# One product of block 1 of the second MLP in the two-level form, with its input fold ahead of the other

## The chip, the cores and the metric

One core of a Trainium2 chip. The metric is the device time of one launch in microseconds (us). The runs of the kernel before gave 652.52 us as their median, between 652.52 and 653.16 us.

## The reference

Attention over 2 x 8 heads (576 positions, head size 64), once on means of 4 neighbouring positions and once on a band of 7, then an MLP with an ELU, then a second MLP with four experts. The change touches only the last:

```python
def _moe2_ref(x, domain_probs, w1, w2) -> np.ndarray:   # x 1152 x 512, w1 4 x 512 x 1024, w2 4 x 1024 x 512
    p = domain_probs / (domain_probs.sum(-1, keepdims=True) + 1e-09)
    for e in range(E):
        h = np.maximum(x @ w1[e], 0.0)
        out += p[:, e:e + 1] * (h @ w2[e])
```

All values are float32. The kernel splits each operand in a high and a low part and takes three matmuls (high x high, low x high, high x low) for one product (`mm3`, L232).

## The kernel before

**Blocks.** The second MLP goes through eight blocks of 512 of the hidden columns, two for each expert. A block n has a first layer (x times a 512 x 512 piece of `w1`) and a second layer (nine token tiles of 128 tokens, `l2e`, which add into `oacc`). The first layer is a Strassen product: seven products of quarter-size matrices. Block 0 has a form of its own (`quad`). From block 1 on the three products numbered 0, 1 and 3 come first, then the remaining ones (`ready`, `last`).

**Two forms of a product.** `plain(n, p)` computes a product of a 2 x 2 arrangement of 128-column pieces directly: four results, each of two `mm3` (6 matmuls of 128x288) in a fresh PSUM bank `psA`, each read once by ScalarE (product 0) or by a VectorE add (products 1 and 3). `inner(n, p)` applies the Strassen form once more: seven groups of one `mm3` (3 matmuls), on three banks: `psA` (called `pa`, four groups accumulate in it one after another), `psB` (`pb`, two groups) and `psC` (one). Between two groups in `pa` VectorE reads what is there so far. `inner` needs the folded input `xq[p]`, made by `fold(p)`: two VectorE sums (L1163), four VectorE differences (L1166), then four results, each a ScalarE copy and a subtraction of VectorE (the first) or GpSimd (L1171); and folded weights, made by `T` (four GpSimd operations, L965 to L968), `H(p, 1)` (a ScalarE copy) and `L(p, 1)` (a GpSimd subtraction). Block 1 has three plain products; block 2 and the later ones have three inner ones, and the folds of 0 and 1 for these are made during block 1. fold() writes its fourth result over a part of its input.

**Order.** Every engine runs its instructions in the order in which the program emits them. Two generators are woven: `weave` takes a step of the first layer at each "m" of a pattern and a step of the second layer's tiles at each "g". A step advances a counter, the emission clock: 0.8 for six matmuls of a product, 0.4 for three, 0.68 for three of a tile. Other work is in a list `due` of (count, function): before each step, all entries whose count is reached are emitted. `plan` puts weight steps in this list: F and F2 (loads), H, L, S, T, HS, LS, H2, L2. The counter starts at 0 with block 0's `quad`s (four of 7 x 0.8, and two tiles of 4 x 0.68 among them), and block 1 follows.

**Buffers.** `s8` is a set of equal SBUF slots, `st_pool[0]` and `st_pool[1]` are single buffers for folded weights, cA, cB and cC hold the sums of the products 0, 1 and 3, and `psb_` has eight PSUM banks given out in turn.

Of the kernel before, what the change touches and what calls it, by code (L numbers as in the profile page):

```python
# [151 lines left out]
def attn_moe_kernel(  # L152
# [794 lines left out]
    def w1_two(n, st_pool):  # L947


        e, s = sbs[n]  # L950
        mine = wm.setdefault(n, ({}, {}))[0]
        c = s * SB
        sub, add = ALU.subtract, ALU.add
        tt = nc.gpsimd.tensor_tensor
        raw, sts = [], {}

        def F():
            raw.append(s8.tile([P, KD, SB], F32, name="raw1", uses=5))
            nc.sync.dma_start(raw[0], w1[e, :, c:c + SB].rearrange("(k p) f -> p k f", p=P))

        def view():
            return raw[0].rearrange("p (h k) (j i f) -> p h k j i f", h=2, j=2, i=2)

        def sums(st, a11, a12, a21, a22):
            tt(out=st[0], in0=a21, in1=a22, op=add)  # L965
            tt(out=st[1], in0=st[0], in1=a11, op=sub)
            tt(out=st[2], in0=a11, in1=a21, op=sub)
            tt(out=st[3], in0=a12, in1=st[1], op=sub)  # L968

        def block(p):  # L970
            h, i = ((0, 0), (1, 0), None, (1, 1))[p]
            return view()[:, h, :, :, i]

        def T(*ps):
            pool = st_pool[0 if len(ps) > 1 else 1]
            st = pool.tile([P, 4, len(ps), P], F32, tag="st", name="st")
            for i, p in enumerate(ps):
                sts["w", p] = st[:, :, i]
            if len(ps) > 1:
                x = view()[:, :, :, :, 0]  # L980
                sums([st[:, o] for o in range(4)], x[:, :, 0, 0], x[:, :, 1, 0], x[:, :, 0, 1], x[:, :, 1, 1])
            else:
                x = block(p)
                sums([st[:, o, 0] for o in range(4)], x[:, 0, 0], x[:, 1, 0], x[:, 0, 1], x[:, 1, 1])

        def parts(p, o):
            w = mine["w", p]
            if o:
                return w[:, 0, 4:8], w[:, 1, 4:8], sts["w", p]
            return [w[:, m, 0:4].rearrange("p (k j) f -> p k j f", k=2) for m in range(2)] + [block(p)]  # L990

        def H(p, o):
            if o == 0:
                mine["w", p] = s8.tile([P, 2, 8, P], F32R, name="wq", uses=1)
            hi, _, x = parts(p, o)
            nc.scalar.activation(hi, x, AF.Copy)  # L996

        def L(p, o):
            hi, lo, x = parts(p, o)
            tt(out=lo, in0=x, in1=hi.bitcast(F32), op=sub)  # L1000
            if o == 0:
                s8.done(raw[0])

        def S(j):
            x = view()[:, :, :, j]
            f0, f1 = [[x[:, h, :, i] for h in range(2)] for i in range(2)]
            for o, a, b, op in (
                (f1[1], f1[0], f1[1], add), (f1[0], f0[0], f1[0], sub), (f0[0], f1[1], f0[0], sub), (f0[1], f0[1], f0[0], sub)
            ):
                tt(out=o, in0=a, in1=b, op=op)  # L1010

        def HS(j):
            mine["s", j] = w = s8.tile([P, 2, KD, 2 * P], F32R, name="ws", uses=2)
            nc.scalar.activation(w[:, 0], raw[0][:, :, 2 * j * P:2 * (j + 1) * P], AF.Copy)  # L1014

        def LS(j):
            w = mine["s", j]
            tt(out=w[:, 1], in0=raw[0][:, :, 2 * j * P:2 * (j + 1) * P], in1=w[:, 0].bitcast(F32), op=sub)  # L1018
            s8.done(raw[0])

        return dict(F=F, T=T, H=H, L=L, S=S, HS=HS, LS=LS)

    with ExitStack() as ph2:
# [130 lines left out]
        def fold(p):  # L1154

            xq[p] = up.tile([P, 3, 2, HB], F32R, tag=f"xq{p}", name="xq")
            buf = cC if p == 3 else up.tile([P, 4, HB], F32, tag=f"xq{2 * p + 1}", name="fold")
            f = buf.rearrange("p (a k) b -> p a k b", a=2)
            f11, f21, f12, f22 = (f[:, a, k] for a in range(2) for k in range(2))
            tt = nc.vector.tensor_tensor  # L1160
            for pair in range(2):
                x = (xbo, xbo, None, xto)[p][pair][:, p].bitcast(F32)
                tt(out=f[:, pair], in0=x[:, 0], in1=x[:, 1], op=add_)  # L1163
                yield
            for o, a, b in ((f11, f12, f11), (f12, f22, f12), (f22, f22, f11), (f21, f21, f22)):
                tt(out=o, in0=a, in1=b, op=sub)  # L1166
                yield
            for k, t in ((0, f11), (1, f22), (2, f12), (3, f21)):
                h, l = xin(p, k)
                cp(h, t)  # L1170
                (nc.gpsimd if k else nc.vector).tensor_tensor(out=l, in0=t, in1=h.bitcast(F32), op=sub)  # L1171
                yield

        def plain(n, p):

            w = wm[n][0]["w", p]
            o = {0: cA, 1: cB, 3: cC}[p]
            for pair in range(2):
                for j in range(2):
                    q_ = 2 * j + pair  # L1180
                    b = bank("psA")
                    for kk in range(2):
                        mm3(b[:, :HB], (w[:, 0, 2 * kk + j], w[:, 1, 2 * kk + j]), xsrc(p, kk, pair), kk == 0, kk == 1)
                    if p == 0:
                        cp(o[:, q_], b[:, :HB])
                    else:
                        add(o[:, q_], cA[:, q_], b[:, :HB])
                    psb_.done(b)
                    if q_ == 3:
                        s8.done(w)  # L1190
                    yield 0.8
# [131 lines left out]
        def join(*gs):  # L1323
            for g in gs:
                yield from g
# [16 lines left out]
        for n, at in ((0, 4), (2, 8), (3, 8.8), (1, 9.6)):  # L1342
            due += [(at, False, lambda n=n: first_xt(n))]
        plan(
# [4 lines left out]
        )  # L1349
        for p, at in (  # L1350
            (0, (28, 28.7, 29.4, 30.1, 30.8, 31.5, 32.2, 32.4, 32.6, 36)),
            (1, (36.5, 37.2, 38, 38.7, 39.4, 40.1, 41, 41.2, 41.4, 45)),
        ):
            due += [(t, False, lambda g=g: next(g)) for g in [fold(p)] for t in at]
        due.sort(key=lambda x: x[0])
# [6 lines left out]
        for n in range(len(sbs)):  # L1362
            m = n + 1
            if n:
                if m < len(sbs):
                    plan(
                        (0, m, "T", 0, 1), (0.5, m, "H", 0, 0), (0.6, m, "L", 0, 0), (4.5, m, "H", 0, 1),
                        (4.6, m, "L", 0, 1), (5, m, "T", 3), (11.6, m, "H", 1, 0), (11.7, m, "L", 1, 0),
                        (11.8, m, "H", 3, 0), (11.9, m, "L", 3, 0), (12, m, "H", 1, 1), (12.1, m, "L", 1, 1),
                        (12.5, m, "H", 3, 1), (12.6, m, "L", 3, 1), (12.7, m, "S", 0), (12.8, m, "S", 1),  # L1370
                        (24.5, m, "HS", 0), (24.6, m, "LS", 0), (25.5, m, "HS", 1), (25.6, m, "LS", 1), (27.5, m, "F2"),
                        (33.5, m, "H2", 0), (33.6, m, "L2", 0), (36.2, m, "H2", 1), (36.3, m, "L2", 1), (36.4, m + 1, "F"),
                    )
                weave(last(n, 0), tiles(n - 1, (6, 7, 8) if n > 1 else (7, 8)), "mgmgmgmgmgmg")
                weave(last(n, 1), tiles(n, (0, 1)), "mgmgmgmgmgmg")
            if m == len(sbs):
                weave(tiles(n, range(2, NTT)), iter(()), "")
                break
            if m == 1:
                pre = join(plain(1, 0), plain(1, 1), plain(1, 3), ready(1))  # L1380
                weave(pre, tiles(0, (2, 3, 4, 5, 6)), "mg" * 20)
                continue
            if m == 2:
                due += [(clock[0] + t, False, lambda g=g: next(g)) for g in [fold(3)] for t in (0, 0.9, 1.8, 2.7, 3.6, 4.5, 5.6, 6.2, 6.8, 7.4)]
                due.sort(key=lambda x: x[0])
                pre = join(inner(2, 0), inner(2, 1), inner(2, 3), ready(2))
                way = "mmmgmmgmggmg" "mmmgmmgmgm" "gmmmgmmgmggm" "mmgmmgmmgmm"
            else:
                pre = join(inner(m, 0), turns(inner(m, 1), inner(m, 3)), ready(m))
                way = "mmmgmmgmggmg" "mmmmgmmgmmgmmgmmgmmg" "mmgmmgmmgmgmg"  # L1390
            weave(pre, tiles(n, (2, 3, 4, 5)), way)
# [32 lines left out]
```

## Time and profile before

| | |
|---|---|
| median of the runs | 652.52 us (652.52 to 653.16) |
| profiled execution, its own time | 652.44 us |
| its span, first to last instruction | 650.6 us |
| TensorE busy | 644.1 us, 99% |
| VectorE busy | 450.3 us, 69% |
| GpSimd busy | 318.3 us, 49% |
| ScalarE busy | 302.9 us, 47% |

Times in the rows below are microseconds from the start of the span. PE is TensorE, PEld its weight loads, DVE VectorE, ACT ScalarE, POOL GpSimd, SPq the queue of SyncE, which issues the loads. A matmul's duration is that of one passage through the array; matmuls overlap, so the distance between the starts of two groups tells what a group occupies. A bracket at the end of a row is the idle time of the engine ahead of it and what ended it.

### The profile page before, as it was taken

The numbers are of one execution on the slowest core, as the hardware profiler recorded it, in microseconds if no ns is written. First come the engines' busy times: TensorE is split into PE (matmuls) and PEld (weight loads), VectorE is DVE, ScalarE is ACT, GpSimd is POOL, SyncE is SP. The second block draws the span as 40 slices with busy tenths as digits, with TensorE's granted clock in tenths as the row PEclk, the third lists the DMA queues.
The fourth block names the chain that finished last, engine by engine and source line by source line (L and its number), as shares of the span: only waits on it lengthen the run. The fifth ranks groups of instructions, "written<-read, shape, count | busy, mean of one in ns | idle before, by whom it ended". The sixth has DMA issues, their size and how long they took to land.

```text
span 650.6 us, 12345 instructions
## 1 busy us (share of the span) xinstructions
PE 644.1 (99%) x4800; PEld 592.2 (91%) x4800; DVE 450.3 (69%) x955; ACT 302.9 (47%) x825; POOL 318.3 (49%) x314
## 2 busy tenths in 40 slices
PE   9999999999999999999999999999999999999998
PEld 5789989999999999999988988988989989989887
DVE  5999999667668883776968666566566565656652
ACT  5999787456564656555323324133142243242110
POOL 5733352303233538386748848538458457376000
PEclk9999999999999999999999999999999999999999
DMA  9999730051141300020220301301102202102012
GB/s 245 220 227 186 168 96 1 2 195 66 65 130 65 130 2 1 2 65 1 65 65 1 129 1 25 106 0 66 66 2 64 66 1 68 62 1 66 1 48 98
DMA packets 40880, 46.70 MB, mean 72 GB/s; under 512 B 23030, under 2 KB 23286, under 8 KB 40822
## 3 DMA queue, kind: packets, MB, share of 16 engines
q1 hardware_dynamic: 40822, 45.91, 25.7%
q8 instruction: 38, 0.62, 0.4%
q14 instruction: 20, 0.16, 0.1%
HBM read 43.55 MB, written 2.36 MB: 71 GB/s over the span
## 4 chain that ended last, share of the span: by engine, by line
PE 87%; DVE 4%; ACT 3%; DMA 3%; POOL 2%; issue 1%; SPq 0%; ACTq 0%; DVEq 0%; POOLq 0%
PE psZ L240 30%; PE psH L240 16%; PE psY L240 14%; PE psE L240 7%; PE psA L240 6%; PE psG L240 3%; PE psF L240 3%; PE psB L240 2%; DMA raw<-in_moe_w_in_dram 2%; DMA raw<-in_k_dram 1%; ACT le L604 1%; PE psC L240 1%; PE psS L585 1%; POOL vtmp L561 1%; PE psX L645 1%
## 5 line engine op out<-in xcount | busy, mean ns | idle before, releaser
L240 PE MATMUL psZ<-wr,h 128*128 128x512 f32 (+2 forms) x876 | 226.8, 390 | 0.0
L240 PEld LDWEIGHTS psZ<-wr,h 128*128 128x128 f32 x876 | 154.4, 188 | 22.1
L240 PE MATMUL psH<-x,w 128*128 128x288 f32 x768 | 107.6, 296 | 0.4 <-DVE w L308 0.3
L240 PE MATMUL psY<-g,w 128*128 128x288 f32 x768 | 105.8, 295 | 0.0
L240 PEld LDWEIGHTS psH<-x,w 128*128 128x128 f32 x768 | 103.2, 188 | 1.7 <-DVE w L308 0.5
L240 PEld LDWEIGHTS psY<-g,w 128*128 128x128 f32 x768 | 103.3, 188 | 0.1
L1138 DVE SCALAR_TENSOR_TENSOR oacc<-psZ,pn,oacc 128x512 f32<-128x512 f32 (+1 forms) x64 | 47.4, 740 | 45.0 <-PE psZ L240 45.0
L826 POOL TENSOR_TENSOR g<-gf,g 128x288 fp32r<-128x288 f32 x26 | 23.0, 887 | 90.3 <-ACT g L821 69.5
L1043 ACT ACTIVATE h<-psF 128x288 fp32r<-128x288 f32 x28 | 11.5, 412 | 118.0 <-DVE psF L1037 118.0
L240 PEld LDWEIGHTS psE<-xt,ws 128*128 128x128 f32 x336 | 48.6, 188 | 3.3
L240 PE MATMUL psE<-xt,ws 128*128 128x288 f32 x336 | 50.6, 295 | 0.0
L1000 POOL TENSOR_TENSOR wq<-raw,wq 128x512 fp32r<-128x512 f32 x21 | 27.0, 1300 | 47.6 <-ACT wq L996 43.4
L400 POOL TENSOR_TENSOR wr<-raw,wr 128x1024 fp32r<-128x1024 f32 x16 | 38.5, 2406 | 21.2 <-ACT wr L395 21.2
L1037 DVE TENSOR_TENSOR c<-psE,c 128x288 f32<-128x288 f32 x56 | 25.4, 457 | 33.5 <-PE psE L240 33.2
L1010 POOL TENSOR_TENSOR raw<-raw 128x256 f32<-128x256 f32 x56 | 42.7, 767 | 3.4
L814 DVE SCALAR_TENSOR_TENSOR gf<-m,psH 128x288 f32<-128x288 f32 x64 | 28.1, 446 | 16.8 <-ACT m L809 12.0
L821 ACT ACTIVATE g<-gf 128x288 fp32r<-128x288 f32 x64 | 27.3, 440 | 25.4 <-DVE gf L814 18.5
L1037 DVE TENSOR_TENSOR c<-psA,c 128x288 f32<-128x288 f32 x62 | 26.6, 455 | 17.6 <-PE psA L240 17.5
L395 ACT ACTIVATE wr<-raw 128x1024 fp32r<-128x1024 f32 x16 | 16.8, 1058 | 43.4 <-DMA raw<-in_moe_w_dram 23.1
L1018 POOL TENSOR_TENSOR ws<-raw,ws 128x1024 fp32r<-128x1024 f32 x14 | 34.1, 2456 | 2.5 <-ACT ws L1014 2.5
L805 ACT ACTIVATE m<-psH 128x288 f32<-128x288 f32 x64 | 25.4, 405 | 19.2 <-PE psH L240 14.5
L308 POOL TENSOR_TENSOR w<-raw,w 128x512 fp32r<-128x512 f32 x12 | 18.5, 1544 | 30.9 <-ACT w L303 30.9
(172 smaller groups left out, 1212.1 us busy)
## 6 DMA issues: line engine op xcount, KB each, us to landing
raw<-in_moe_w_dram SPq DMA_DIRECT2D x16, 1024.0 KB, 5.2
raw<-in_moe_w_in_dram SPq DMA_DIRECT2D x8, 1024.0 KB, 7.5
raw<-in_moe_w_out_dram SPq DMA_DIRECT2D x8, 1024.0 KB, 5.0
vb<-in_v_dram SPq DMA_DIRECT2D x16, 160.0 KB, 8.0
vraw<-in_v_dram SPq DMA_DIRECT2D x4, 576.0 KB
out_dram<-oacc SPq DMA_DIRECT2D x8, 256.0 KB, 2.0
raw<-in_k_dram SPq DMA_DIRECT2D x2, 576.0 KB, 7.5
raw<-in_q_dram SPq DMA_DIRECT2D x2, 576.0 KB
```

The source lines that it names most:

```text
L240: nc.tensor.matmul(ps, wt[a], xt[b], start=first and n == 0, stop=last and n == 2, skip_group_check=more)
L308: ENG[eng].tensor_tensor(out=t[:, 1, r], in0=up.bitcast(F32), in1=t[:, 0, r].bitcast(F32), op=ALU.subtract)
L400: nc.gpsimd.tensor_tensor(out=t[:, 1], in0=raw[0][:, 2 * j:2 * j + 2], in1=t[:, 0].bitcast(F32), op=ALU.subtract)
L805: nc.scalar.activation(m, ps1["h", s, t, f][:, :HB], AF.Relu, scale=-1.0)
L814: nc.vector.scalar_tensor_tensor(out=gf, in0=m, scalar=-1.0, in1=ps[:, :HB], op0=ALU.add, op1=ALU.max)
L821: nc.scalar.activation(g[:, 0], ps1["gf", s, t, f], AF.Copy)
L826: ENG[eng].tensor_tensor(out=g[:, 1], in0=gf, in1=g[:, 0].bitcast(F32), op=ALU.subtract)
L1000: tt(out=lo, in0=x, in1=hi.bitcast(F32), op=sub)
L1010: tt(out=o, in0=a, in1=b, op=op)
L1018: tt(out=w[:, 1], in0=raw[0][:, :, 2 * j * P:2 * (j + 1) * P], in1=w[:, 0].bitcast(F32), op=sub)
L1037: nc.vector.tensor_tensor(out=o, in0=y, in1=x, op=add_)
L1138: nc.vector.scalar_tensor_tensor(out=a, in0=ps, scalar=sc, in1=a, op0=ALU.mult, op1=ALU.add)
```

## The change

Block 1's product 1 goes from `plain` to `inner` and comes last of the three; products 0 and 3 stay plain. Its folded weights are made by T at 12, H and L of the folded part follow those of the plain part at 17.2 and 17.3. fold(1) takes the due counts that fold(0) had, and fold(0) those of fold(1). fold(1) works in cB, and fold(0) in the buffer that later holds `xq[3]`. A single-block T goes to the first of the two weight buffers for products 0 to 2. The weave pattern of block 1 gets one more "m" pair in the stretch of the new product.

```diff
         def T(*ps):
-            pool = st_pool[0 if len(ps) > 1 else 1]
+            pool = st_pool[0 if ps[0] < 3 else 1]
...
         def fold(p):
-            buf = cC if p == 3 else up.tile([P, 4, HB], F32, tag=f"xq{2 * p + 1}", name="fold")
+            buf = {0: None, 1: cB, 3: cC}[p] or up.tile([P, 4, HB], F32, tag="xq3", name="fold")
...
         plan(
-            (0, 1, "F"), (9.5, 1, "H", 0, 0), (9.6, 1, "L", 0, 0), (17, 1, "H", 1, 0), (17.1, 1, "L", 1, 0),
+            (0, 1, "F"), (9.5, 1, "H", 0, 0), (9.6, 1, "L", 0, 0), (12, 1, "T", 1), (17, 1, "H", 1, 0), (17.1, 1, "L", 1, 0), (17.2, 1, "H", 1, 1), (17.3, 1, "L", 1, 1),
...
         for p, at in (
-            (0, (28, 28.7, 29.4, 30.1, 30.8, 31.5, 32.2, 32.4, 32.6, 36)),
-            (1, (36.5, 37.2, 38, 38.7, 39.4, 40.1, 41, 41.2, 41.4, 45)),
+            (1, (28, 28.7, 29.4, 30.1, 30.8, 31.5, 32.2, 32.4, 32.6, 36)),
+            (0, (36.5, 37.2, 38, 38.7, 39.4, 40.1, 41, 41.2, 41.4, 45)),
...
             if m == 1:
-                pre = join(plain(1, 0), plain(1, 1), plain(1, 3), ready(1))
-                weave(pre, tiles(0, (2, 3, 4, 5, 6)), "mg" * 20)
+                pre = join(plain(1, 0), plain(1, 3), inner(1, 1), ready(1))
+                weave(pre, tiles(0, (2, 3, 4, 5, 6)), "mg" * 8 + "mmgmgmmgmg" + "mg" * 8)
```

## Rows read from the trace of the kernel before

**Rows 1.** The page's first part: busy us, share of the span, instructions.

```profile
PE 644.1 (99%) x4800; PEld 592.2 (91%) x4800; DVE 450.3 (69%) x955; ACT 302.9 (47%) x825; POOL 318.3 (49%) x314
```

**Rows 2.** Windows in block 1: length, each engine's busy us, granted clock, DMA, GB/s.

```profile
310.00:316.00 6.00, 6.00 (x38) 5.44 (x37) 5.86 (x9) 1.86 (x5) 4.15 (x3) 1.00 0.33 81
316.00:322.00 6.00, 6.00 (x38) 5.43 (x37) 5.97 (x9) 1.39 (x2) 4.03 (x3) 1.00 0.24 94
322.00:328.00 6.00, 6.00 (x38) 5.43 (x37) 5.28 (x12) 2.73 (x6) 4.93 (x4) 1.00 0.00 0
```

**Rows 3.** TensorE's waits, total, times, longest: longest of all; 300 to 370 us.

```profile
PE psW L928 <- DVE junk L897: 0.9, 1, 0.9
...
PE psA L240 <- DVE c L1037: 0.2, 1, 0.2
```

**Rows 4.** Timeline of TensorE (start, us, instructions): block 1's third product; block 2.

```profile
315.95 0.96 PE L240 MATMUL psA<-xt,wq 128*128 128x288 f32 x6
316.75 0.87 PE L240 MATMUL psZ<-wr,h 128*128 128x512 f32 x3
317.45 0.96 PE L240 MATMUL psA<-xt,wq 128*128 128x288 f32 x6
...
358.08 0.55 PE L240 MATMUL psA<-xbo,wq 128*128 128x288 f32 x3
358.48 0.56 PE L240 MATMUL psB<-xq,wq 128*128 128x288 f32 x3
```

**Rows 5.** Timeline of VectorE in block 1, 319 to 325 us.

```profile
319.39 0.74 DVE L1136 TENSOR_SCALAR oacc<-psZ,pn 128x512 f32<-128x512 f32 x1
320.05 2.17 DVE L1166 TENSOR_TENSOR fold<-fold 128x288 f32<-128x288 f32 x1
322.15 0.45 DVE L1037 TENSOR_TENSOR c<-psA,c 128x288 f32<-128x288 f32 x1
322.52 0.44 DVE L1166 TENSOR_TENSOR fold<-fold 128x288 f32<-128x288 f32 x1
322.88 1.09 DVE L1171 TENSOR_TENSOR xq<-fold,xq 128x288 fp32r<-128x288 f32 x1
323.89 1.18 DVE L1037 TENSOR_TENSOR c<-psA,c 128x288 f32<-128x288 f32 x3
```

**Rows 6.** Timeline of GpSimd, 316 to 325 us (the last: second of two).

```profile
316.31 1.32 POOL L1171 TENSOR_TENSOR xbo<-fold,xbo 128x288 fp32r<-128x288 f32 x1
319.51 2.40 POOL L400 TENSOR_TENSOR wr<-raw,wr 128x1024 fp32r<-128x1024 f32 x1 [1.88 <-ACT wr L395]
322.85 1.80 POOL L1171 TENSOR_TENSOR xq<-fold,xq 128x288 fp32r<-128x288 f32 x2 [0.93 <-ACT xq L1040]
...
323.62 1.03 POOL L1171 TENSOR_TENSOR xq<-fold,xq 128x288 fp32r<-128x288 f32 x1
```

**Rows 7.** Timeline of TensorE and VectorE in block 2.

```profile
356.89 0.67 PE L240 MATMUL psA<-xbo,wq 128*128 128x288 f32 x3 [0.21 <-DVE c L1037]
...
356.39 0.44 DVE L1037 TENSOR_TENSOR c<-psA,c 128x288 f32<-128x288 f32 x1
```

**Rows 8.** Timeline of GpSimd and ScalarE, weight steps; SyncE's wait, 300 to 330.

```profile
342.58 0.46 POOL L965 TENSOR_TENSOR st<-raw 128x128 f32<-128x128 f32 x1
...
295.81 2.55 POOL L1000 TENSOR_TENSOR wq<-raw,wq 128x512 fp32r<-128x512 f32 x2 [4.21 <-PE psZ L240]
298.44 6.36 POOL L1010 TENSOR_TENSOR raw<-raw 128x256 f32<-128x256 f32 x8
307.26 5.49 POOL L1018 TENSOR_TENSOR ws<-raw,ws 128x1024 fp32r<-128x1024 f32 x2 [2.46 <-ACT ws L1014]
...
295.11 1.14 ACT L996 ACTIVATE wq<-raw 128x512 fp32r<-128x512 f32 x2
306.12 1.06 ACT L1014 ACTIVATE ws<-raw 128x1024 fp32r<-128x1024 f32 x1
...
SPq L959 <- POOL wr L400: 8.6, 1, 8.6
```

## The prediction

> **What bounds the kernel now.** I read the page's busy line first: TensorE is busy for 99% of the span [rows 1]. So a change pays only by the TensorE time it takes out, and costs only where TensorE comes to stand still. Next I read the windows over block 1: in each, TensorE is busy for all 6.00 us at a granted clock of 1.00 (its 2.4 GHz level), and VectorE, at 5.86 of 6 us and then 5.97, is as full as TensorE [rows 2]. The waits of TensorE say how little stands still: 0.2 us in 300 to 370 us, and 0.9 us as the longest single wait of the whole run [rows 3]. Last come the timelines of the two engines over the same stretch. TensorE issues the product of block 3 from 315.95 us [rows 4]; VectorE reads the first result of that product at 322.15 us [rows 5]. **VectorE is thus about 5 us behind.** TensorE does not feel it, because a plain product writes each result to a PSUM bank of its own and goes on to the next. That is the cover which the change takes away.
>
> **Removed.** Block 1's product 1 takes 7 groups of 3 matmuls instead of 4 groups of 6: 21 against 24. Six matmuls of this shape occupy TensorE from 315.95 to 316.75 us, 0.133 us each [rows 4]; a group of 3 takes 0.40 us in block 2, which already has the two-level form [rows 4]. Saved: 3 x 0.133 = **0.40 us**, all of it on the path. VectorE gains three adds (7 for 4) at a spacing of 0.37 us [rows 5], 1.1 us.
>
> **Added weights.** T for block 1 is four 128x128 GpSimd operations (0.46 us [rows 8]), 1.8 us in all, issued at counter 12. They find GpSimd in the 4.21 us that it waits ahead of 295.81 us [rows 8]. H(1,1) is one more ScalarE copy like the two that follow each other at 295.11 us (1.14 us for both, so 0.6 us more [rows 8]); its reader L(1,1) is behind L(1,0) anyway. L(1,1) is one more 128x512 subtraction, 2.55/2 = 1.28 us [rows 8], between L(1,0) and L(3,0). It pushes the eight sums S from an end at 304.80 to 306.1 us. Their readers, the two ScalarE copies of `ws`, run from 306.12 us on [rows 8], and GpSimd had 2.46 us free ahead of 307.26 us [rows 8], so nothing later moves. Without that cover each microsecond would go on to the `ws` split, which ends at 307.26 + 5.49 = 312.75 us; TensorE wants it at 315.95 + 4 x 1.5 = 321.95 us, a pair of steps being 0.80 + 0.70 [rows 4]. I take zero.
>
> **Moved.** fold(1) takes the places in the list that fold(0) had, and the other way round: the same 7 VectorE, 4 ScalarE and 3 GpSimd instructions at the same counts. fold(1) now works in cB, which nothing in block 1 has written by then. Its four results are there when fold(0)'s are today, the last at 316.31 + 1.32 = 317.6 us [rows 6]; the group that reads the last one comes after 321 us, and the first group that reads any, at 316.35 us, needs VectorE's, which is the earliest. Product 3 goes second; its weights are split by about 300 us even with L(1,1) ahead. No load is moved past another: block 2's F waits for the split of `wr` on GpSimd (8.6 us [rows 8]), not for the slot of the last product's weights. Zero again.
>
> **The added wait, and where I put the price.** In `inner`, three results accumulate one after another in the bank `pa`: VectorE must have read `pa` before TensorE may add the next group to it. Block 2 shows this: the `psA` group at 356.89 us waits for the add that began at 356.39 us and took 0.44 us, so TensorE starts 0.06 us after VectorE ends [rows 7].
>
> Which add, and when does VectorE get to it? I count the emission clock: block 1 begins at 4 x 5.6 + 2 x 2.72 = 27.84; eight "mg" pairs of 1.48 bring it to 39.68, where `inner` begins. Fold(0)'s steps due at 36.5, 37.2, 38, 38.7 and 39.4 are issued by then, before the add of the first group. That is exactly the place where the first add of block 3's product stands today, behind the step that begins at 320.05 us. That step, a subtraction that takes 0.44 us when free, took 2.17 us: GpSimd was splitting `wr` from 319.51 to 321.91 us, and the step ended 0.3 us after [rows 5, 6]. Nothing ahead of it is changed, so I expect VectorE's rows to be the same up to 322.15 us, where now the add on `pa` begins.
>
> TensorE from 315.95 us: groups `pa`, `pb` (0.40 each), a tile part (0.70 [rows 4]), the `psC` group, a tile part: the second group on `pa` is due at 318.55 us. It can go at 322.15 + 0.45 + 0.06 = 322.66 us. **First pause 4.1 us.** Behind it in TensorE's order stand all other products and tiles; there is nothing else to run.
>
> The third group on `pa` is due 0.40 + 0.40 + 0.70 later, at 324.16 us. It needs the next add on `pa`, and ahead of that VectorE has: the add on `pb` (0.37), fold steps 6 and 7, the add on `psC` (0.37). Steps 6 and 7 read SBUF alone, and two GpSimd subtractions run from 322.85 to 324.65 us [rows 6]. In the trace of before, step 7 met the first of them and took 1.09 us [rows 5]. Now step 6 stands there and step 7 meets the second: VectorE at 322.89, 323.9 and 324.9, the `psC` add to 325.27, the `pa` add to 325.72 us. **Second pause** 325.78 - 324.16 = 1.6 us. If neither step is held (0.37 each) it is 0.35 us; if GpSimd's second split of `wr`, as long as the first (2.40 us [rows 6]), starts at 324.65 us ahead of step 7, it is 324.65 + 2.40 + 0.3 + 0.37 + 0.45 + 0.06 - 324.16 = 4.1 us. I take 1.6, the row of step 7 being the nearest. The fourth group on `pa` is then just in time.
>
> Sum: 4.1 + 1.6 - 0.4 = +5.3 us. Against the profiled execution's 652.44 us (span 650.6, 1.84 around it; the median of the runs, 652.52, is 0.08 above), **657.7 us**, 0.8% slower. Ends: 652.44 + 4.1 + 0.35 - 0.4 = 656.5; 660.2 with the large second pause.
>
> What of TensorE's clock? Every window here has it at 1.00, also behind the longest wait, 0.9 us [rows 2, 3]; no row shows a pause of 4 us. The Trainium skill, page "TensorE: Matmul & The Clock Gate", section "What's actually happening", says that the low clock is the default state and that activity releases it, so that an idle stretch can bring it back. By it the sum would grow by what a low stretch costs (the second rival); without it the sum stays at +5.3 us.
>
> **Rivals.** (1) **No pause**: VectorE reaches the add on `pa` by 318.0 us, or the group doesn't have to wait; then only the 0.40 us is left, 652.0 us, not slower. For it: before has no wait at all in this stretch with the same lag. Against: block 2's wait [rows 7], and VectorE, which would have to be over 4 us earlier with the same list ahead of it. It decides at an add that starts by 318.04 us. (2) **The clock falls** in the first pause. At 1.2 GHz each group takes twice as long; if that holds for as long as the pause, 4.1 us of work at half speed lose 2.05 us, less what the second pause absorbs (up to 1.6). 658.2 to 659.8 us, I name 659.5. For: the pause is over four times the longest here. Against: no window of the trace under 1.00. (3) **The hold falls elsewhere**: the load of `w2` lands a little later or earlier, so that GpSimd's split doesn't catch step 5. Then the add on `pa` starts at 320.42 and the pause is 2.4 us; the split holds step 6 instead, until about 322.2, and the second pause is about 1 us: 652.44 + 3.4 - 0.4 = 655.4 us. For: step 5 began only 0.54 us after the split. Against: the load hangs on the same chain as before.
>
> **How the numbers follow.** Forecast 0.68; rival 1 0.08; rival 2 0.12; rival 3 0.10; a gain of more than 1.3 us, for which I find no mechanism, 0.02. The range 654.5 to 660.3 holds the forecast with its bounds and rivals 2 and 3, leaving out 0.10 and little more for their edges. A measurement of this kernel can tell about 0.2%, 1.3 us, from no change: rival 1's 0.4 us is "same". Faster 0.02, same 0.08, slower 0.90.
>
> **What would show it.** In the profile after: 4797 matmuls; a `psA` group near 322.7 us with some 4 us idle ahead, ended by VectorE's add, and a second one near 325.8 us; VectorE's step at 320.05 us still long beside GpSimd's `wr`; T near 291.6 us; everything behind block 1 shifted by one constant. Wrong: no idle `psA` group in 318 to 327 us (rival 1), a granted clock under 1.00 behind the pause (rival 2), a short step 5 (rival 3), or a wait of ScalarE for the sums S, which would put the cost on the added weights instead.

## The result and the profile after

| | before | changed |
|---|---|---|
| median of six runs each | 652.60 us | 658.23 us (656.74 to 658.73) |
| ratio | 1 | 1.0083 (95% interval 1.0070 to 1.0096) |
| profiled execution, span | 650.6 us | 655.8 us |

The changed kernel is slower by 5.6 us in the median, where 5.3 had been forecast; the profiled execution, at 657.71 us, is 5.3 us above that of before (652.44 us). Its profile shows where. First the page: three matmuls fewer than in [rows 1], and one slice of the granted clock that is not 9.

```profile
PE 645.3 (98%) x4797; PEld 592.5 (90%) x4797; DVE 451.8 (69%) x958; ACT 303.4 (46%) x826; POOL 321.2 (49%) x319
PEclk9999999999999999999899999999999999999999
```

The windows over block 1 of the changed kernel (length; busy us and instructions of PE, PEld, DVE, ACT, POOL; granted clock; DMA share, GB/s) answer to [rows 2]:

```profile
310.00:316.00 6.00, 6.00 (x38) 5.43 (x37) 5.86 (x9) 1.86 (x5) 4.14 (x3) 1.00 0.26 89
316.00:322.00 6.00, 2.53 (x15) 1.92 (x13) 5.97 (x10) 1.40 (x3) 3.81 (x3) 1.00 0.22 86
322.00:328.00 6.00, 5.53 (x22) 4.29 (x23) 5.36 (x10) 2.56 (x6) 5.12 (x4) 0.72 0.02 2
```

Up to 316 us both kernels are alike. Then TensorE is busy for 2.53 of 6 us while VectorE stays full, and in the next window the clock averages 0.72. Behind that the two are the same again: 312 us from 328 us on in the kernel before, and 312 us from 333.4 us on in the changed one, have equal TensorE time.

```profile
328.00:640.00 312.00, 311.79 (x1789) 278.56 (x1788) 193.22 (x421) 94.72 (x198) 169.77 (x159) 1.00 0.14 45
```

```profile
333.40:645.40 312.00, 311.79 (x1789) 278.50 (x1789) 192.79 (x421) 94.67 (x198) 168.20 (x158) 1.00 0.12 42
```

So all of the loss lies in a few microseconds. TensorE's timeline there (start, us, instructions, idle time ahead and its releaser) shows the new product: the first group on `pa`, the tile part ahead of the second, the second, and the groups behind it down to the first of `ready`:

```profile
315.79 0.56 PE L240 MATMUL psA<-xbo,wq 128*128 128x288 f32 x3
...
317.67 0.86 PE L240 MATMUL psZ<-wr,h 128*128 128x512 f32 x3
322.47 1.06 PE L240 MATMUL psA<-xq,wq 128*128 128x288 f32 x3 [3.94 <-ACT xq L1040]
323.32 0.92 PE L240 MATMUL psB<-xbo,wq 128*128 128x288 f32 x3
324.05 1.48 PE L240 MATMUL psZ<-wr,h 128*128 128x512 f32 x3
325.48 0.64 PE L240 MATMUL psA<-xq,wq 128*128 128x288 f32 x3
...
327.93 0.96 PE L240 MATMUL psE<-xt,ws 128*128 128x288 f32 x6
```

The second group was due at 317.67 + 0.70 = 318.37 us and goes at 322.47: a pause of 4.1 us (3.94 us by the bracket, which counts from the modelled end of the tile part). Then three groups take 3.01 us (322.47 to 325.48) where 0.40 + 0.40 + 0.70 = 1.5 would do. VectorE over the same time (the first row is step 5 of fold(0); the second is the add on `pa` that the pause waits for, the last the next add on `pa`):

```profile
319.89 2.07 DVE L1166 TENSOR_TENSOR fold<-fold 128x288 f32<-128x288 f32 x1
321.88 0.44 DVE L1037 TENSOR_TENSOR c<-psA,c 128x288 f32<-128x288 f32 x1
...
322.61 1.01 DVE L1166 TENSOR_TENSOR fold<-fold 128x288 f32<-128x288 f32 x1
323.55 1.06 DVE L1171 TENSOR_TENSOR xq<-fold,xq 128x288 fp32r<-128x288 f32 x1
324.52 0.45 DVE L1037 TENSOR_TENSOR c<-psC,c 128x288 f32<-128x288 f32 x1
324.89 0.44 DVE L1037 TENSOR_TENSOR c<-psA,c 128x288 f32<-128x288 f32 x1
```

Down to the first add they are the rows of before [rows 5], 0.2 to 0.3 us earlier on this span; behind it the new adds are set in between. The add ends at 322.32 us, 0.15 us ahead of TensorE's group. And GpSimd, with the split of `wr` beside step 5 and the two fold subtractions beside steps 6 and 7, as in [rows 6]:

```profile
319.30 2.34 POOL L400 TENSOR_TENSOR wr<-raw,wr 128x1024 fp32r<-128x1024 f32 x1 [1.84 <-ACT wr L395]
322.51 1.78 POOL L1171 TENSOR_TENSOR xq<-fold,xq 128x288 fp32r<-128x288 f32 x2 [0.87 <-ACT xq L1040]
```

The profile names ScalarE's copy into `xq` as the releaser of the pause, because that copy ended last (322.44 us). It is a copy of fold(0), which the group does not read. In two of the experiments below (steps 6 to 10 behind, and both) this copy stands behind the group in the program, so that the group can't wait for it, and the group still goes 0.14 us after VectorE's add.

What the forecast had in another place is the granted clock, here in single microseconds (busy us, clock, DMA):

```profile
321.00:322.00 1.00, 0.00 (x0) 1.00 0.00 0
322.00:323.00 1.00, 0.53 (x2) 0.51 0.00 0
...
324.00:325.00 1.00, 1.00 (x5) 0.50 0.00 0
325.00:326.00 1.00, 1.00 (x6) 0.78 0.00 0
```

Late in the pause, near 322.0 us, the granted clock falls to TensorE's 1.2 GHz level and stays there until about 325.5 us; all three groups of the second loss run at it. Both the low clock and VectorE's next add (it ends at 325.33 us) would make the third group on `pa` late. Which of them does is the question that the profile alone leaves open.

### The profile page after: what moved, and what is told of

Same layout as the page of the kernel before. It is cut to its first block, busy times and chain, and to the rows that moved or that the text cites. A ratio compares the mean times of both kernels' runs of the same rounds, so it can differ in the third digit from the quotient of the medians.

```text
span 655.8 us, 12351 instructions
## 1 busy us (share of the span) xinstructions
PE 645.3 (98%) x4797; PEld 592.5 (90%) x4797; DVE 451.8 (69%) x958; ACT 303.4 (46%) x826; POOL 321.2 (49%) x319
## 3 DMA queue, kind: packets, MB, share of 16 engines
HBM read 43.55 MB, written 2.36 MB: 70 GB/s over the span
## 4 chain that ended last, share of the span: by engine, by line
PE 85%; DVE 8%; ACT 3%; POOL 1%; issue 1%; DMA 1%; SPq 0%; ACTq 0%; DVEq 0%; POOLq 0%
PE psZ L240 29%; PE psH L240 16%; PE psY L240 14%; PE psE L240 7%; PE psA L240 5%; PE psG L240 3%; PE psF L240 3%; PE psB L240 2%; DMA raw<-in_k_dram 1%; PE psC L240 1%; PE psS L585 1%; POOL vtmp L561 1%; ACT le L604 1%; PE psX L645 1%; DVE c L1163 1%
## 5 line engine op out<-in xcount | busy, mean ns | idle before, releaser
L1000 POOL TENSOR_TENSOR wq<-st,wq 128x512 fp32r<-128x512 f32 x19 | 24.4, 1299 | 20.4 <-ACT wq L996 20.4
```

## The experiments

My theory: VectorE, behind because of fold(0), releases `pa` 4 us late, and later once more; GpSimd's operations lengthen VectorE's SBUF-only steps. Rivals: the product's chain of groups through one bank costs the time by itself; the low clock causes the second loss; the added weights cost something.

The group that opens the new product starts between 315.23 and 316.63 us in these profiles, so the table counts from it. All its stretches are read from the rows shown in this section and the one above, and each kernel's rows are those of one profiled execution. Several intervals of the ratios overlap, so the medians alone can't rank the variants; the stretches show where each differs.

| kernel | first to second `pa` group | second to third | third to first `psE` | sum | median, ratio to before |
|---|---|---|---|---|---|
| changed | 6.68 | 3.01 | 2.45 | 12.14 | 658.23, 1.0083 |
| fold(0) behind the product | 2.58 | 1.48 | 2.36 | 6.42 | 652.40, 1.0001 |
| pause filled | 6.59 | 3.03 | 2.44 | 12.06 | 657.64, 1.0080 |
| steps 6 to 10 behind | 6.55 | 2.86 | 2.62 | 12.03 | 658.30, 1.0086 |
| both | 6.78 | 1.57 | 2.36 | 10.71 | 656.12, 1.0052 |
| GpSimd's split behind | 5.06 | 3.02 | 2.44 | 10.52 | 656.56, 1.0056 |

**fold(0) behind the product.**

```diff
-            (0, (36.5, 37.2, 38, 38.7, 39.4, 40.1, 41, 41.2, 41.4, 45)),
+            (0, (45.5, 46.2, 47, 47.7, 48.4, 49.1, 50, 50.2, 50.4, 54)),
```

> The changed kernel with one edit: all ten steps of fold(0) are due after the new product (45.5 to 54 instead of 36.5 to 45). My theory: the pause comes from VectorE's lag behind fold(0), so the first add on pa runs near 317 us, no psA group waits, TensorE's clock stays at 1.00 and only the 3 saved matmuls are left: 652.5 - 0.4 = 652.1 us. Rival (the two-level form itself, with its three groups chained through one bank, costs the time wherever fold(0) lies): still a pause of some us, 656 to 658 us.

Measured: 652.40 us, ratio 1.0001 (0.9988 to 1.0014), span 650.1 us. TensorE and VectorE:

```profile
315.93 0.56 PE L240 MATMUL psA<-xbo,wq 128*128 128x288 f32 x3
...
318.51 0.56 PE L240 MATMUL psA<-xq,wq 128*128 128x288 f32 x3
...
319.99 0.55 PE L240 MATMUL psA<-xq,wq 128*128 128x288 f32 x3
...
322.35 0.96 PE L240 MATMUL psE<-xt,ws 128*128 128x288 f32 x6
```

```profile
317.58 0.44 DVE L1037 TENSOR_TENSOR c<-psA,c 128x288 f32<-128x288 f32 x1
```

The first `psE` group of the kernel before, which closes the same stretch there:

```profile
321.95 0.96 PE L240 MATMUL psE<-xt,ws 128*128 128x288 f32 x6
```

The add runs at 317.58 us, the second group goes without a wait, and the whole loss is gone. The rival that the two-level form costs the time by itself falls. The gain of 0.4 us can't be told from no change in the median.

**Filling the pause.** 18 matmuls into a bank that nobody reads, so that TensorE works while it waits.

```diff
+            if n == 1:
+                jk = bank("psJ", uses=0)
+                for _ in range(18):
+                    nc.tensor.matmul(jk, identb, junk.to_broadcast([P, 512]), start=True, stop=True)
             go(pa, 5, xin(p, 1), False)
```

> The changed kernel with 18 extra matmuls of 128x512 bf16 ahead of the second group on pa, into a bank that nobody reads, so that TensorE works through most of the 4.1 us pause. Both theories: the granted clock stays at 1.00 and the first pause ends at the same add, near 322.4 us. If the low clock (0.50 from 322 to 325.8 us in the changed kernel) is what delays the third group on pa, that group now runs near 324.0 us and the time is 1.5 us below the changed kernel's, 656.7 us. If VectorE's add, which ends at 325.33 us, delays it as well, it still runs near 325.4 us and only the slower groups behind it are won back: 657.9 us.

Measured: 657.64 us, ratio 1.0080 (1.0058 to 1.0102). TensorE, and the granted clock:

```profile
316.63 0.56 PE L240 MATMUL psA<-xbo,wq 128*128 128x288 f32 x3
...
319.21 4.09 PE L1219 MATMUL psJ<-junk,identb 128*128 128x512 bf16 x18
323.22 0.63 PE L240 MATMUL psA<-xq,wq 128*128 128x288 f32 x3
...
326.25 0.63 PE L240 MATMUL psA<-xq,wq 128*128 128x288 f32 x3 [1.30 <-ACT h L1043]
...
328.69 0.96 PE L240 MATMUL psE<-xt,ws 128*128 128x288 f32 x6
```

```profile
323.00:327.00 4.00, 2.69 (x16) 1.00 0.00 0
```

The clock stays at 1.00, and now the third group stands still for 1.30 us until VectorE's add. Without the low clock the second loss is as large as with it (3.03 against 3.01 us). The median, 0.6 us lower, can't be told from that of the changed kernel.

**Steps 6 to 10 of fold(0) behind the product.**

```diff
-            (0, (36.5, 37.2, 38, 38.7, 39.4, 40.1, 41, 41.2, 41.4, 45)),
+            (0, (36.5, 37.2, 38, 38.7, 39.4, 45.1, 45.6, 45.8, 46, 46.6)),
```

> The changed kernel with fold(0)'s steps 6 to 10 due behind the new product (45.1 to 46.6), steps 1 to 5 as they are. The first pause stays at 4.1 us. Now VectorE's second add on pa is ready by about 323.7 us. If VectorE's steps 6 and 7 set the second loss, TensorE's third group on pa runs near 324.0 us and the time is 656.7 us. If the low clock suffices to delay it, the group runs near 325.5 us as in the changed kernel and the time stays at 658 us, with the clock at 0.50 for some 3.5 us.

Measured: 658.30 us, ratio 1.0086 (1.0063 to 1.0109). TensorE; VectorE's second add on `pa` and its steps 6 and 7; and the clock:

```profile
315.23 0.56 PE L240 MATMUL psA<-xbo,wq 128*128 128x288 f32 x3
...
321.78 1.06 PE L240 MATMUL psA<-xq,wq 128*128 128x288 f32 x3 [3.82 <-ACT xq L1040]
...
324.64 0.81 PE L240 MATMUL psA<-xq,wq 128*128 128x288 f32 x3
...
327.26 0.96 PE L240 MATMUL psE<-xt,ws 128*128 128x288 f32 x6
```

```profile
322.95 0.46 DVE L1037 TENSOR_TENSOR c<-psA,c 128x288 f32<-128x288 f32 x1 [0.58 <-PE psA L240]
...
327.21 0.45 DVE L1166 TENSOR_TENSOR fold<-fold 128x288 f32<-128x288 f32 x1
327.57 0.45 DVE L1171 TENSOR_TENSOR xq<-fold,xq 128x288 fp32r<-128x288 f32 x1
```

```profile
323.00:324.00 1.00, 1.00 (x5) 0.50 0.00 0
324.00:325.00 1.00, 1.00 (x4) 0.50 0.52 47
```

VectorE's add is ready at 323.41 us, over a microsecond ahead, and TensorE is busy throughout: the low clock alone now holds the third group, and the time stays. Steps 6 and 7 take 0.45 us each here, where GpSimd is idle from 325.02 to 328.21 us; in the changed kernel, beside GpSimd's two subtractions, they took 1.01 and 1.06 us.

**Both edits together.**

> Both edits of the two runs before together: the 18 extra matmuls in the pause and steps 6 to 10 of fold(0) behind the product. Each of the two causes by itself hides the other; with both gone the third group on pa should run near 324.0 us at clock 1.00, and of the loss only the first pause less the 0.4 us saved is left: 652.5 + 4.1 - 0.4 = 656.2 us, 1.5 to 2 us below the changed kernel. If it stays at 658 us, something else holds the groups apart.

Measured: 656.12 us, ratio 1.0052 (1.0031 to 1.0072), 2.1 us below the changed kernel in the median and 1.4 us in the stretch (10.71 against 12.14).

```profile
316.58 0.56 PE L240 MATMUL psA<-xbo,wq 128*128 128x288 f32 x3
...
323.36 0.63 PE L240 MATMUL psA<-xq,wq 128*128 128x288 f32 x3
...
324.93 0.55 PE L240 MATMUL psA<-xq,wq 128*128 128x288 f32 x3
...
327.29 0.96 PE L240 MATMUL psE<-xt,ws 128*128 128x288 f32 x6
```

With neither cause left, the three groups take 1.57 us. So the second loss of 1.4 us has two sufficient causes that lie over each other; taking away one shows nothing. What is left is the first pause.

**GpSimd's splits of the second layer's weights behind the product.**

```diff
-            ... (37.1, 1, "L2", 0), (42.1, 1, "L2", 1), ...
+            ... (45.6, 1, "L2", 0), (45.7, 1, "L2", 1), ...
```

> The changed kernel with GpSimd's two splits of block 1's second-layer weights (L2) due behind the new product, at 45.6 and 45.7 instead of 37.1 and 42.1; everything else as it is. If VectorE's step 5 of fold(0) took 2.07 us because GpSimd was at that split, it now takes 0.45 us, the first add on pa begins near 320.3 us, the first pause is 2.4 instead of 4.1 us; steps 6 and 7 still meet GpSimd's two fold subtractions, so the second loss stays near 1.6 us, and the time is 652.5 + 2.4 + 1.6 - 0.3 = 656.2 us. If step 5 is slow by itself, nothing changes: 658 us.

Measured: 656.56 us, ratio 1.0056 (1.0039 to 1.0072). TensorE, VectorE's step 5 and the clock:

```profile
315.96 0.56 PE L240 MATMUL psA<-xbo,wq 128*128 128x288 f32 x3
...
321.02 0.64 PE L240 MATMUL psA<-xq,wq 128*128 128x288 f32 x3 [2.31 <-ACT xq L1040]
...
324.04 0.64 PE L240 MATMUL psA<-xq,wq 128*128 128x288 f32 x3 [1.28 <-ACT h L1043]
...
326.48 0.96 PE L240 MATMUL psE<-xt,ws 128*128 128x288 f32 x6
```

```profile
320.06 0.45 DVE L1166 TENSOR_TENSOR fold<-fold 128x288 f32<-128x288 f32 x1
```

```profile
317.00:323.00 6.00, 3.44 (x18) 1.00 0.04 14
323.00:329.00 6.00, 4.96 (x29) 1.00 0.30 83
```

Step 5 takes 0.45 instead of 2.07 us once GpSimd is not at a split, and the first stretch is 1.6 us shorter. 1.6 of the 4.1 us were thus GpSimd's operation lying on VectorE's step; the other 2.5 us stand without it. The clock stays at 1.00 through pauses of 2.3 and 1.3 us, and the second loss, now VectorE's alone, is again 1.5 us.

**The added weights alone.** All of block 1's products plain, in the old order and weave, with T, H and L made and the folds swapped. fold(1)'s last step reads cB after the plain product has written it, so one folded result of product 1 differs from block 2 on; the amount of the work is not touched, and of its order only that step is.

```diff
-            (1, (28, 28.7, 29.4, 30.1, 30.8, 31.5, 32.2, 32.4, 32.6, 36)),
+            (1, (28, 28.7, 29.4, 30.1, 30.8, 31.5, 32.2, 32.4, 32.6, 45)),
...
-                pre = join(plain(1, 0), plain(1, 3), inner(1, 1), ready(1))
-                weave(pre, tiles(0, (2, 3, 4, 5, 6)), "mg" * 8 + "mmgmgmmgmg" + "mg" * 8)
+                pre = join(plain(1, 0), plain(1, 1), plain(1, 3), ready(1))
+                weave(pre, tiles(0, (2, 3, 4, 5, 6)), "mg" * 20)
```

> The change without its new product: all of block 1's products plain and in the old order and weave, but with T, H and L of product 1's folded weights made (and not used) and with fold(1) ahead of fold(0), fold(1)'s last step due at 45, behind the plain product that still reads its input. If the added weight steps and the swapped folds cost nothing, as I worked out, the time is the kernel before's, 652.5 us within 0.6. If GpSimd's 3.1 us more or the swap cost something, up to 3 us more.

Measured: 652.53 us, ratio 0.9995 (0.9982 to 1.0008). GpSimd's added L(1,1) and its wait ahead of the `ws` split:

```profile
297.05 1.29 POOL L1000 TENSOR_TENSOR wq<-st,wq 128x512 fp32r<-128x512 f32 x1
...
307.23 5.50 POOL L1018 TENSOR_TENSOR ws<-raw,ws 128x1024 fp32r<-128x1024 f32 x2 [1.24 <-ACT ws L1014]
```

The split begins where it began before; only GpSimd's idle time ahead of it went from 2.46 to 1.24 us [rows 8]. VectorE's lag here is the same as before (the first add of product 3 begins at 322.25 us, before at 322.15), and no group waits, because every plain result has its own bank.

## Why the prediction was right, point by point

- **VectorE's lag as the cover that goes away: right.** Moving fold(0) out from in front of the adds takes away all of the loss; the lag without a shared bank (the added weights alone) costs nothing.
- **First pause: 4.1 us forecast, 4.1 measured.** It was read off the place that the first add of block 1's product 3 ("the product of block 3" in the prediction) had in VectorE's rows. The hand-over from VectorE to TensorE was put at 0.06 us from one row of block 2; in the five kernels with a pause it was 0.14 to 0.15 us. That the sum still came out is in part luck: step 5 was 0.10 us shorter than before (2.07 against 2.17).
- **GpSimd's hold on step 5: right.** Without the split the step takes 0.45 us. Rival 3 had put its worth at 1.7 us less in the first pause; the run gave 1.6. Its 1 us for the second loss assumed a split that holds step 6 instead; in this run no split did, the fold subtractions held steps 6 and 7 as in the changed kernel, and the loss was 1.5 us.
- **Second pause: 1.6 us forecast, 1.5 measured, with one more cause than forecast.** Steps 6 and 7 took 1.01 and 1.06 us as foreseen and the add on `pa` came when foreseen. But TensorE was not standing still until then: it was working at half the clock.
- **The clock: rival 2's event came, its price did not.** I gave the fall a chance of 0.12; the profile shows it behind the pause, and the mean granted clock is 0.994 to 0.997 in all six runs of the changed kernel. The sum that rival 2 wrote down, a low stretch less what the second pause absorbs, had the right form, and its lower end, 2.05 - 1.6 = 0.45 us, was still too much: the low stretch lasted some 3.5 us, but mainly the three groups up to the next add run in it, and their 1.5 us more is time in which TensorE would have waited. The fall cost about 0.1 us in the stretch (12.14 against 12.06). The Trainium skill, page "TensorE: Matmul & The Clock Gate", section "What's actually happening", by which the low clock is the default state and activity releases it, agrees as to the fall itself: 0.50 behind a pause of 4.1 us.
- **The median: 657.7 us forecast, 658.23 measured; the 0.5 us stay open.** The measured median lies where rival 2 had its lower end, but the stretch doesn't bear rival 2's price out. The profiled execution, with a mean clock of 0.997, took 657.71 us, and its low stretch behind the pause accounts for that mean. Three of the six runs have 0.994 or 0.995 and took 658.40 to 658.73 us, so they had more low clock; no profile of the changed kernel shows where. The profile of the filled kernel has such a stretch far from the new product, 0.50 from 11 to 13 us.
- **The saving: 0.40 us forecast, 0.3 measured in the stretch.** In the kernel before, the product with the same five tile parts takes 321.95 - 315.95 + 0.70 = 6.70 us, the 315.95 and the 0.70 for its fifth tile part from [rows 4]; with fold(0) out of the way 6.42. The fourth group still comes 0.1 us late behind the third add, which the prediction had called just in time.
- **Added weights and swapped folds at zero: right**, 0.9995 (0.9982 to 1.0008).

## What to carry to other kernels

A kernel whose TensorE never waits can still have another engine 5 us behind, covered by free PSUM banks. Before results are chained through one bank, read from the trace when the reading engine gets to each result today; the difference to TensorE's own time was the larger part of the price here, 4.1 of 5.6 us. Move the reading engine's other work behind the chain, or leave the product in the form with a bank for each result.

## What the runs showed of the hardware

- In two profiles an idle time of TensorE of 3.94 and 3.82 us went with a fall of the granted clock to 0.50 for about 3.5 us; idle times of 2.31 and 1.28 us in a row left it at 1.00. A long pause is not the only way there: in the filled kernel the clock was at 0.50 from 11 to 13 us, and TensorE's waits up to there were two of 1.3 us together and one of 0.9 us.
- The low clock cost 0.1 us in the stretch, since the next result that TensorE needed was late anyway. Two such causes over one another can't be found by taking away one of them: the three groups took 2.86 and 3.03 us with one gone, 1.57 with both.
- A VectorE subtraction of two SBUF operands that began 0.6 us after the start of a GpSimd split of 2.34 us took 2.07 us, and 0.45 us where GpSimd was not at the split, while VectorE's adds with an operand in PSUM took 0.44 to 0.46 us beside GpSimd's second split, from 324.25 us on.
